# An attention and expert kernel whose recorded order of operations is replaced by one meant to keep VectorE's shared-port steps clear of GpSimd's steps

## Chip, cores, metric

One core of one Trainium2 chip. The metric is device time of one execution in microseconds (us); lower is better. Kernel before: 264.78 us, median of 3 runs (264.57 to 265.2).

## The reference, cut to what matters

```python
mod = (silu(c) @ w_mod).reshape(1, 6, 1, 576)            # sa, ca, ga, sb, cb, gb
h = layernorm(x) * (1 + ca) + sa                          # x: 1 x 2048 x 576
# 32 heads of width 18, 4 segments of 512 tokens:
for s in range(4):
    p = softmax(qs @ ks.T * scale + causal_mask)          # exponentials on ACT
    a_mem = (phi(qs) @ M) / (phi(qs) @ z + 1e-6)          # phi(t) = t + 1 if t > 0 else exp(t)
    o = g * a_mem + (1 - g) * (p @ vs)
    M, z = M + phi(ks).T @ vs, z + phi(ks).sum()
x = x + ga * (o @ wo)
h = layernorm(x) * (1 + cb) + sb
r = h @ w_r;  best = argmax(r)                            # one token of 2048 goes to the expert
y = (silu(h[best] @ w_gate) * (h[best] @ w_up)) @ w_down * sigmoid(r[best])
out = x + gb * (h + scatter(best, y))
```

Attention fills most of the time; the expert on one token (weights of 576 x 4608) is the tail, because the token is known only when all 2048 have been scored.

## The kernel before: the parts that matter

The kernel first writes down some 1650 operations with what they read and write, then emits them in a recorded order. A number in that order says which operation comes next and which of its alternatives (engines) is taken. Semaphores follow from what is read and written; nothing but its place in its own engine's queue keeps an operation back when its data is there.

```python
    def recorded(self):
        raw = base64.b85decode(BANKS)
        for g, b in zip(self.groups(), raw):              # PSUM banks of each group
            g.banks = [b] if g.n == 1 else [b // 8, b % 8]
        raw = base64.b85decode(ORDER)
        seq = []
        for x in struct.unpack("<%dH" % (len(raw) // 2), raw):
            o = self.ops[x // 4]
            o.eng, _, o.emit = o.alts[x % 4]              # x % 4: the engine chosen
            seq.append(o)
        return seq
```

The steps in dispute, all between operands in SBUF:

```python
    def tt(out_, a_, b_, o_, R, W, pool=False):           # residual and modulation steps
        if pool:
            return op(one("POOL", 1.3, lambda: nc.gpsimd.tensor_tensor(...)), ...)           # L912
        op(alts(("DVE", ..., lambda: nc.vector.tensor_tensor(out=out_, in0=a_, in1=b_, op=o_)),    # L913
                ("POOL", 1.3, lambda: nc.gpsimd.tensor_tensor(out=out_, in0=a_, in1=b_, op=o_))))  # L914
    ...
    ts_ = ...tensor_scalar(PH, QT, 1.0, 1.0, op0=ALU.add, op1=ALU.max)   # L698, VectorE, one SBUF input
    mn_ = ...tensor_tensor(out=PH, in0=PH, in1=EQK, op=ALU.min)          # L700, VectorE, two SBUF inputs
    # L559: normalisation on VectorE (L558 on GpSimd); L931: sum of the two attention parts
    # L787: affine_select, GpSimd, causal mask on the exponentials (L776, ACT)
```

In the tail, `xcols` (L1240 to L1242, three VectorE steps of up to 6 columns) makes the input of the expert's matmuls (L1259) from what the selecting matmuls left in PSUM.

## Time and profile before

| before | value | where it is read |
|---|---|---|
| time | 264.78 us (264.57 to 265.2) | the runs |
| span of the profiled run, mean granted clock of PE | 264.4 us, 0.928 | the list of cores |
| first exponential starts, last ends | 32.6, 234.8 us | L776 in ACT's timeline |
| ACT idle between them | 20.9 us of 202.3 | the same |
| VectorE port steps held by over 0.1 us | 31 of 87, 20.0 us in sum | each step's time less the fastest of its shape |
| of that on the chain that ended last | 9.6 us (from 144.7 us on) | chain of waits |
| PE at half clock | 38.3 us in 7 stretches | granted clock, within the span |

"Port steps" are VectorE's steps between operands in SBUF. A step's held time is its time less the fastest of its line and shape; "on the chain" is what of that lies on the chain of work that ended last. "Half clock" is time with a granted TensorE clock of 0.50. "Held" and "on the chain" are worked out by one rule for all kernels here, the fastest being taken over both kernels; by the prediction's rule, which took the kernel before alone, the first is 19.5 us.

For the comparison I cut the span in four at the work, not at the clock: up to the first exponential, to the 113th of 160, to the end of the last, and the rest. These are the busy times of the kernel before by those stretches (start and end of the stretch, its length, then busy us and instructions of PE, PE loads, VectorE, ACT, GpSimd; granted clock; DMA share; GB/s):

```profile
0.00:32.60 32.60, 27.78 (x225) 14.28 (x228) 22.91 (x87) 12.37 (x24) 13.17 (x38) 0.84 0.77 217
32.60:169.70 137.10, 130.19 (x1836) 76.90 (x1852) 119.80 (x268) 130.19 (x158) 87.34 (x109) 1.00 0.58 183
169.70:234.80 65.10, 54.88 (x1098) 34.33 (x1098) 57.18 (x144) 51.10 (x62) 45.73 (x72) 0.84 0.62 185
234.80:264.40 29.60, 19.46 (x386) 12.10 (x385) 17.37 (x68) 6.65 (x19) 14.21 (x23) 0.87 0.59 209
```

The profiled run took 266.25 us, 1.5 over the median. The second stretch is ACT's: 130.2 of 137.1 us. In the third no engine is full; VectorE comes nearest, with 57.2 of 65.1 us, 9.1 of them held.

### The profile page before, as it was taken

What the parts mean: (1) busy time and instruction counts of PE and PEld (TensorE: products, weight loads), DVE (VectorE), ACT (ScalarE), POOL (GpSimd) and SP (SyncE); (2) the same over time, 40 slices, a digit from 0 to 9 for tenths busy, and PEclk for the clock granted to TensorE, in tenths of its full rate; (3) what the DMA queues carried; (4) which work ended last, traced back from release to release, by engine and by line L of the source; (5) the groups of instructions that cost most, each with busy time, mean ns of one, the idle gap of its engine ahead of it and who ended that gap; (6) DMA issues with size and microseconds to landing.
All of it is one profiled execution on the core that took longest, in us unless ns stands there. A gap on an engine that the chain in (4) does not pass through costs nothing. (4 is left out here: it accounts for less than half of the span.)

```text
span 264.4 us, 8893 instructions
## 1 busy us (share of the span) xinstructions
PE 232.3 (88%) x3543; PEld 137.6 (52%) x3562; DVE 217.3 (82%) x564; ACT 200.3 (76%) x257; POOL 160.5 (61%) x240
## 2 busy tenths in 40 slices
...
ACT  2232999999997988999999999968757995774020
...
PEclk9858999999999999999999999997777995899689
...
GB/s 172 321 186 273 142 222 124 149 233 259 139 183 150 146 100 247 110 145 141 139 152 327 252 132 260 249 135 137 210 219 49 271 260 191 135 297 298 140 326 3
DMA packets 35263, 50.38 MB, mean 191 GB/s; under 512 B 4043, under 2 KB 29266, under 8 KB 35222
## 3 DMA queue, kind: packets, MB, share of 16 engines
...
q10 hardware_dynamic: 544, 0.59, 0.7%
...
HBM read 37.93 MB, written 11.87 MB: 188 GB/s over the span
## 5 line engine op out<-in xcount | busy, mean ns | idle before, releaser
L776 ACT ACTIVATE arena<-PS 128x1024 bf16<-128x1024 f32 x160 | 152.3, 1037 | 11.5 <-PE PS L758 6.6
L787 POOL TENSOR_SCALAR_AFFINE_SELECT arena<-arena 128x1024 bf16<-128x1024 bf16 (+1 forms) x59 | 57.6, 987 | 47.5 <-ACT arena L776 45.5
L645 PE MATMUL PS<-arena 128*128 128x512 bf16 (+1 forms) x176 | 50.9, 391 | 1.5 <-issue 0.9
L758 PE MATMUL PS<-arena 18*128 18x128 bf16 (+2 forms) x736 | 37.7, 266 | 3.2 <-DVE arena L810 0.9
L950 PE MATMUL PS<-arena 128*128 128x288 bf16 x160 | 30.3, 313 | 2.0 <-DVE arena L943 1.0
L758 PEld LDWEIGHTS <-arena 18*128 18x128 bf16 x736 | 16.1, 94 | 26.6 <-issue 23.7
L802 PE MATMUL PS<-arena 128*32 128x128 bf16 (+2 forms) x736 | 25.5, 269 | 4.3 <-issue 2.5
L712 PE MATMUL PS<-arena 128*128 128x288 bf16 x160 | 28.1, 292 | 0.3 <-issue 0.2
L914 POOL TENSOR_TENSOR arena<-arena 128x576 bf16<-128x576 bf16 x20 | 26.5, 1329 | 2.4 <-DVE arena L913 1.9
L645 PEld LDWEIGHTS <-arena 128*128 128x128 bf16 (+1 forms) x195 | 17.8, 103 | 16.8 <-issue 6.0
L802 PEld LDWEIGHTS <-arena 128*32 128x32 bf16 x736 | 14.3, 98 | 14.9 <-issue 8.5
L551 POOL TENSOR_TENSOR mv<-mv,epsF 128x1 f32<-128x1 f32 (+2 forms) x21 | 4.1, 194 | 26.9 <-DVE mv L544 25.9
L558 POOL TENSOR_SCALAR arena<-arena,rstd,nmr 128x576 bf16<-128x576 bf16 x19 | 17.0, 897 | 5.4 <-DMA arena<-in_A_x_dram 4.5
L649 DVE CAST arena<-PS 128x512 bf16<-128x512 f32 (+1 forms) x26 | 17.5, 681 | 3.1 <-DMA arena<-in_A_x_dram 1.1
L950 PEld LDWEIGHTS <-arena 128*128 128x128 bf16 x160 | 14.9, 105 | 9.3 <-issue 1.9
L810 DVE CAST arena<-PS 128x512 bf16<-128x512 f32 (+1 forms) x26 | 17.2, 663 | 1.9 <-PE PS L802 1.6
L913 DVE TENSOR_TENSOR arena<-arena 128x576 bf16<-128x576 bf16 x25 | 18.0, 736 | 0.1
L712 PEld LDWEIGHTS <-arena 128*128 128x128 bf16 x160 | 13.8, 98 | 7.6 <-issue 2.2
L542 DVE BATCH_NORM_STATS2 st<-arena 128x6 f32<-128x288 bf16 x30 | 13.6, 452 | 4.6 <-DMA arena<-in_A_x_dram 4.5
L964 DVE SCALAR_TENSOR_TENSOR arena<-PS,arena 128x288 bf16<-128x288 f32 x32 | 14.2, 447 | 3.3 <-PE PS L953 3.1
L695 ACT ACTIVATE arena<-arena 128x1024 bf16<-128x1024 bf16 (+1 forms) x18 | 16.6, 924 | 0.0
L552 POOL TENSOR_TENSOR rstd<-mv,mhalf 128x1 f32<-128x1 f32 (+2 forms) x21 | 13.5, 644 | 4.2 <-DVE mhalf L407 2.7
...
## 6 DMA issues: line engine op xcount, KB each, us to landing
...
```

Of the source, the lines that this page charges most:

```text
L558: a = {"POOL": ("POOL", 0.83, lambda: nc.gpsimd.tensor_scalar(dst, src, sc_, bi_, op0=ALU.mult, op1=ALU.add)), "DVE": ("DVE", 0.43, lambda ...
L645: nc.tensor.matmul(bank(g, 0)[0:r], lhsT=lhs(k), rhs=h1T[hb][:, k, :], start=(k == 0), stop=(k == KC - 1))
L649: op(alts(("DVE", dv(512, "P"), lambda g=g, dst=dst, r=r: nc.vector.tensor_copy(dst, bank(g, 0)[0:r])), ("ACT", ac(512), lambda g=g, dst=d ...
L712: nc.tensor.matmul(bank(g, 0)[:, 0:288], lhsT=h1T[hb][:, k, 128 * b:128 * b + 128], rhs=WP["v"][:, k, 288 * hf:288 * hf + 288], start=(k = ...
L758: nc.tensor.matmul(bank(gs_[x // 2], x % 2)[:, off:off + b - a], lhsT=KS[32 * x:32 * x + DH, c, 128 * j:128 * j + 128], rhs=QS[32 * x:32 * ...
L776: op(one("ACT", 1.035, lambda g=gs_[x], pt=pt: nc.scalar.activation(pt, pair(g), ACT.Exp, scale=SCALE)), R=[("lt", n)], W=[("PT", pp, x)], ...
L787: om = op(alts(("POOL", 0.68 if pat[0][1] == 4 else 1.12, lambda v4=v4, pat=pat: nc.gpsimd.affine_select(out=v4, in_=v4, pattern=pat, comp ...
L802: nc.tensor.matmul(bank(gp, 0)[32 * x:32 * x + 32, o0 + a - qa:o0 + b - qa], lhsT=va[:, j, 4 * c + x, :], rhs=PT[:, pp, x, off:off + b - a ...
L810: ("DVE", dv(w, "P"), lambda gp=gp, ai=ai, gi=gi: nc.vector.tensor_copy(ASB[ai][:, gi, 0:w], bank(gp, 0)[:, 0:w]))),
L913: op(alts(("DVE", dv(576, acc=2), lambda: nc.vector.tensor_tensor(out=out_, in0=a_, in1=b_, op=o_)), ("POOL", 1.3, lambda: nc.gpsimd.tenso ...
L914: ("POOL", 1.3, lambda: nc.gpsimd.tensor_tensor(out=out_, in0=a_, in1=b_, op=o_))), R=R, W=W, lock=True)
L950: nc.tensor.matmul(bank(g2[hf], 0)[:, 0:288], lhsT=ot[:, k, :], rhs=wop[:, k, 288 * hf:288 * hf + 288], start=(k == 0), stop=False)
```

## The change

Its intent: order all operations so that no VectorE step that uses the port shared with GpSimd is due while a GpSimd step runs. Only the two tables change; of the operations common to both, 151 also change engine (117 of them are five masks, five steps on GpSimd that become 112 small matmuls on PE; 34 are others), the PSUM banks change, and 55 filling matmuls become 44. The tables cannot be read by eye:

```diff
 ORDER = (
-    "001-qOaKS~cmO;A&;Wn{lmM6j<p2Z#gaLp7Pyh@7d;rw|Z~$BY*#I~IKmnWpi~$e;XaH0Iv;n*UxB=||%mJVPqyVS@hyjcMumF$&lmVClzyZVo$N|s+gaAbV"
     ... (34 more lines out)
+    "00A@rOaM>-cmP}g=m2m4d;kalgaPCL3;>J)Kmd>dJOESxfC01txB<KY%mI`E1OPYzH~`Q9U;vl_005i-hykDgqyP{A%mAnWAOOGt$N{hb#Q`t?)Bw-{6aZuZ"
     ... (all lines of the table new)
 BANKS = (
     ... (9 lines changed)
```

More of the change, by code (lines that the diff above doesn't have):

```diff
@@ L35 @@
 ORDER = (
-    "001-qOaKS~cmO;A&;Wn{lmM6j<p2Z#gaLp7Pyh@7d;rw|Z~$BY*#I~IKmnWpi~$e;XaH0Iv;n*UxB=||%mJVPqyVS@hyjcMumF$&lmVClzyZVo$N|s+gaAbV"
-    "K>!p0xB$EWtN@$=+ySHkpaH-D=>YHm^Z<weU;yv|SODw+v;g%1I02{uAOK_lpaawaumRWs7zf}1paM7o=>cd0%m91=+yIaO<pBf(+yZO@AP2+%JObbXPy(a_"
-    "xC00StOGCrqykg|r~;@1umeB>90#oe$N*RZMFOk=a0284bpl-iBnMyu3<HD$7y|eK90CyoxB_?r=>qHm2m&Aiv;zzR_yQCIB?9~ayaU7oC<4F(5CTX7C<puj"
-    "ECK)m6#_5<1p?3m$ODK1OaqJpYydR^_ybS_WCP#;8~~95AOlnbFb8M@00d+LBm+zW*aQ3nZ38?3EC)0P+yf{Bhyy?almkQq-~&kmm;;>yj05NcI0r-r>;v!v"
@@ L40 @@
-    "!~$>w$O0?_kpp}K%mVZS1Oz<?fCC5wlmbBqTn9-9umXhx3<P`v&;now5Cmig<O56xPzP8CbOU$;SOe4oNB~s_Tm$$3oB~J$C;(ss00C?Vv<z?uzzk>ybO%rb"
-    "m;xvSfC5Ye90^neybLV_SOg#mTm-xVxC~$fBni+5zyf#(83Z5%6a@SNd<duq)Ca^2fCwA}I0J+T*axf!XaukaFaz8NB?Qn6Gy{+av<Ex`Fa&S}Yy^k|ln2QS"
-    "*aDCQ^b8mSH3Vb?_y?E=j08LcI0VfMbOiVeoCp03v;sf`{0Ddh;0Htm1Oe~@fCS6~m;{{!cn5q0@CTp>bN~Pd1PG)E*aY+f)C|}R;0zQ9d<X0Ypa-Z37zp$S"
-    "+zi|VhzNuPfCq#J-~^Netq8aTyad1qpaj4K!~_5XEC3_`=nVJ><P01L<OEa*r34`eL=wmZJQ7$4tOV=~KoY0~%miEr7y$eT&;+;#)C8~u2m$d7BnSZs)B|7$"
@@ L44 @@
-    "v;+(R7y;-6@C57x;0Txn<Omc2oCSyn2nFZ}C<QPD4FwznFbJRps09!KECr+mGzhE(_yqg}I0#V^JP5D_v;_bK7!7O)a0na$BmwLQ1PSy6O%fapKnNfKR1!D^"
-    "JOv;P1O-e15D6p=C;=!9@CXzM2nqBEbO<mFKn27H3<(egNCh|&Gz~Nb6$MNMSPf7G$OnuE7zxY=NC7wvxDB`kNC><Q#0AI&JPlX{m<UV=zy)OiECEOoPzYQN"
-    "U<JSp&;`5&%mrW#)CDjBWDTSTj0ju>01ccCya+S_Xa#TuWC%nB1PyEjbOpo>01hk&)Cf=kKn(~8#0X#kpbfkS*a(ye=n8xi2n|>P-3Z7C><VlFY!b`}coNYF"
-    "bPdQ2R0XgIqz!NZkO-*_1P<^D^a^MVfDLH@3=L=!_zGMSoCsJFff6VNbO9g>2oC%TVG<|~<Og^GbrOUP3=4=2ObuiO3=Sv@WD>LzB@5^Wzz1*=Eej9}6bp?F"
@@ L48 @@
-    "EDit*1Pd?@H4YdHkPR>k2n!txcm*g4cnviR+zr$XxDrqeeFfkRFbNP2d=0!3I0-BX5D4TAfCa!3oD!@J=nXsxg$4KxKnYY0^bH^m><x$oNE3_&NC`{{kOh<l"
-    "pb|s~OcOK-q!OqSqz)Vf7zI!XAO%DTs1DE#XbCVA5DichG!twIC<r743<wAqa0#pqR0(tmv<OracnMeuTnRW6NDJ5vU<o`6*adwFI13CIKnp|*JQFMpObZ+i"
-    "Y!g%q+y&qTtP*4is0pwMEC#p;Fb1p%a1;CufC<P6g$Z;MTn>y0&<S7;coWzO%n4);hzTSP>;>cn+zIdn;0cfklnGD^=mh`<nF%xoXb3z8^aY>^{RKD%_yxHM"
-    "2nL)9I1WVyzzMVolnqD*)Cs%^#R)(LPzK})r3pw53<iu26b(cUh!c<wj1$NPO$Jy7C<>Jh=m~rVkP~<Y?FoPe6caECFdPU9Q~@js3<@*~7!wc*5e66rs1TGB"
@@ L52 @@
-    "tPmU%@CmRD#1i!hTm~ElArr6=j0QjxND5F2ObYlCkOo)_U<R}hd=sDs{1R9bR0f>}7zzLrgc8gK1QQ$zR0@a^I0_&N&<0Qrj1pW6NDW*8kP?^^m<@ymBnngx"
-    "JPKG2Kne&G%ngVJcnTB>m<Id__z8Rp019XhxDad(bPfaxl?Fr#SPFm&ybxdtaSo^oTnexX)CPDCs0L*UtP0o$m=1gnxC$T!L=Bt{a19g&@C{53X$HUwZ3YAe"
-    "pbpRy)DpA`m<reuyb9<BoC<^rtOlS8<p$ga;0B2bkP5^Kj0$WG+!CM=?FRS;U<;%Ql?v<<XbON1Yznjugbwfqhz`&Su@1NnloI>~^ai95)e6W8v<@^JI2=42"
-    "zz)a`%?jKK*a~n8bP7NmL>x#QOdL=g&<?N$;0ojl#17C9WD95uYzrg?%n&>d3=H%a+z`kR#1PaD_!j^N@D4x@*bcxDWCr*S<QHHJ2?x{=%no=9;1X~Py$-kr"
@@ L56 @@
-    ";SPKYBolB3^bUy&bPEj!=nmWt<PPl)j0?;cfeQc+Ko3X{{0@W*L=U6}xeI&{fDnWbyasdz6b`ftR2;kua1eA5$Pxq(Fb{YT2oE?9zzYozU=R2c{1X5a)Dx5o"
-    "02mk!G!JACArIISXb;^JBoCMph!Bhr%nK+FEe|{okPy%d;0xUgzy??xTpUmj5Dyd&7!Sk?R1e4tkPi?C=n@<c*bvwY2n<94)eD#loeNA4uo7?&SPz&FY!3_*"
-    "U>vXybr0+lln>+*Tn_{o#0KaK><hFH@DuzO%o2DH@C)<{!4DJ%xDWIb5Da|}fDaT5#1F_1gb%zEoDZZ6h!5lopbx+kqz{Y_#1mW$WDFn-WE=nxXbdC_Gz`2C"
-    "F$}2-s1Fzn1P~ky(GRo+tPkK1`3nRG2oTs0DGaa^EDSsh<qx0>)DIvKv=g`!-48$v%?~6HtqTkgln^Kom=Nd>oDg&jXdDp`U=#fd0Sp)r?GNx0MGVjvYz!<A"
@@ L60 @@
-    "6cBg}WD|u9a11dJL=!X+I1q>o@DGp+^bc$ta2#|TK@da`ToX(T$P<7J9S}$m_zzJG{0~qN1Ppx)kPPS$RS+-~I24QwG!)De&=ar=C=>J&O%Od0SP)$h1QZ|?"
-    "Bot^9lngu(2o!`9WDpP&U=R!xcpQ8j5fnHKXb@}=><}mv6cpeSoD8HB<P+!<NDP1+fE1_`@DQLA7!(~8h!o%u<Pf9`^bn{FgdB(*j2r+F1QApWU=%DApbUf*"
-    "lo9w4XcVjyOcp#85fKy-K@m_EWEA`mR2D!ML>534oD(b)j1)u^a1;p<*cV6^m=Qz~coeM+=@D!cWEMyioDmEWbQF9PND*ijY!*xu5E#G|#1u>s$P`o&P!Zr4"
-    "kP#daSP^Iu7!h0%AQ9vdWf8CxxD>P$%oJ1<U=dIhkQ7)HToh~(>=9TDm=q)tfD@DyoD}g9C=pl|kQ~tza1qoLTozy!+!v%2ED@*?pcJSS*c7Z0)E6NYC>5*}"
@@ L64 @@
-    "m<*s1q!GLnxe)*ryb&Z7>=!K+@D~Ub-4t{Yc@gvxv=Olp1QqBMF%hr~_z@8mG!cLi?G)e?Ko}Gi^b`mZ3>Ewl1rit)9Tnvi@DyPc#1Z%u{1h-1=ofquWEE%?"
-    "H5C975E2a%Z52@!6c{)a#1=gjSQS7OR23K!lpL5GL=~JBpcP0JOch-fg%NZW$PsWAcom!+pd6$ej1_Peq!oY_bQX9P$QH~N%n{HLd=)qm)e(Fah!zwQ*b&?j"
-    "fEI)m&=!;xkQE>oh!u<$7#P42m==i<j1im`gcjftkQUe#91<WB;1wJfBp2Kj)E3+p*cOx);1=u_Bod$&s1<k@C>O~U%oU^-<rXOtm=*9A=oa`E<Q1?LtQDvn"
-    "tQ@c$1s2d12o~%W3>Nejs20@~=oPgU@f9o=5f&sExD~t=6&4s4z!e-8#1$|XAr|x%{1yNg_!TG^ED{742p9Yn02VYCNEl2QKo?LLd>1SjI2S}0Bo-(ZR2Z}z"
@@ L68 @@
-    "fEP#?EEY5tFcvr#JQq9`g%_+ASQs%9h!>F;loy#7To|wxj2BQBR2K~wU>KYiq!+jss289YtQS}pTo=3-uot)-yd1zB#2m;R%p7bOz!!uV#23gH&>Ykp*c{v("
-    ";2h)}=p1kubQob5>>ThM^c?sc{2Txs1RZ=BfEW-LI2h;{G#E4zco;+&WEf}|q!_doxE4$o6c@Y}JQ!pbv=;~+oEV50z!oqVpct$es2Cg=AQ)*E>=^VIZ5Qwu"
-    "j2IXfkQkI0a2IqJ_!#^cuo$!$xEQ<`z!=0B%oxxZ$Qaxh*cj9p;27i>02u@s2pO0d3>g")
-BANKS = (
-    "2LK8N2L%8J1O^2H00RaG0S5yI0S5p80R{jHB?=`sB@-naE(Zq(6D1`994;;a0WJap1OYAzE&(njHxnfR2LLw{0VO2?0WKT?0S5vD1OWjY1_c5H009F71p);H"
-    "0R{jE0s#jE1ONa60|W;E2Ll2F1~(iW0Rbfe6AC2<1_L)769E$?B>^`90ssOf6E_?IB{u;I90dXaB{v*5Hwpna95(<40099v0RjdB03`+m1O*2N2Lb~E0|EjE"
-    "0|f>K0t5yJ0s;d90ssU81_B2YB{wA#B>^`RHv$3z0UQB0Hyi;j95(_40UQA(H!cA#6E`IT0|F%h0XGUIB{u;j2Lu2d0WLQH0S5sA0tW&D0s{mB0|NsG1qTBK"
-    "1_b~B1_lEM2LJ#D0tW{L2MQb$E&&q+0|o&cE&(n92Lb{m0VOvjHvj+zHzf)s0VM<k0xkgo69)$_0RbEU023|&E(Ze&911rB023|&0RjR90|x{H1q25I00#g8"
-    "0RaF32R8sE0RR91000000000000000000000000000000000000000000000000000000000000000000000000000000000000000000000000000000000"
+    "00A@rOaM>-cmP}g=m2m4d;kalgaPCL3;>J)Kmd>dJOESxfC01txB<KY%mI`E1OPYzH~`Q9U;vl_005i-hykDgqyP{A%mAnWAOOGt$N{hb#Q`t?)Bw-{6aZuZ"
@@ new lines @@
+    "fB>ujgaGgWqyg{&>;aqsL;&mnJONk$v;f!vpaHl5)B*JY+yUSLPy+k_hybVo<N??KgaT*+paa|h+yaaMI0C!?zyQPm$N=B~d;w?xBnRmM-~ylmKmoV|1OXri"
+    "umP+AkN{Ky90!O3qyjtw<N~MyYyzzUKmu?Abpludi~{rk!~z%xqyt?72m+A;7y_sRMFO}2_yMc~cmfOpumijU`~mm?5CXshlmh7j$O8ZZ1p;6K90C;rNCGGV"
+    "AOb7`=mRAJFao>+$N~fd!~-Y?%mOR`fC2~uAOl1J_yW)ZoB}lhOad$ilmqMo@B<73m;?9&v;#l`L<1xPWC9Tbd;-)0oC7om`~#Q*83aiKhy#oR8~`u}^aIQT"
+    "C<E*Q00bNaAOw&DECV<Pd;{16fCGdBWCPp-XanE_Yy$`cKnF|%5Cm8QJO^+CumVK~3<OXEzye7JbOT%iU<Y^uB?Mdt1Ozk#<O37~NCa#LR0CiGXa`UPa0g@u"
@@ new lines @@
+    "Oax2^xC}4@PzMwQC<HJBR0k{s5E-}xzyw$a&;zIkI0UQ*bO$vAzzjG8JOr=@Km@!5L<D#Q*aEZ%fCLBud<3)t3;}2aYy?>Za0I*z6aoAKkO!0i_y}ACU<8-|"
+    "ln0mxi3E%UJOgC}kOY+k00R&KYyflw{0OuRoCg32R0Nm=)C1rMBml?+$qdW{pa+Bm#01a;<OrPv&<yAZcnF{b)C3p-=mhKpr3CN<d<ex1907O-&<A`6^a6kg"
+    "fCq&L*aRp5-~`+R5DC-=ga^$G*bLYQ+y~SQ6bRi6;0$yC_yimStOWD~7y~E)s08o=umrROxCa;r<OKW#00oE#ECD0|6bTp!90(x@BnaRKya)IUj0Xq>NCor^"
+    "1O*KR<P01M_y<r0Oa+(){0!&}@CTd)5Cv!jGy(hv><1tT@C<AP><kqJBnbcra0LVi^alh97!4QzL=rFvI0Y~PumuPSC<w#{Gzhc>JOw}n91RQ!I0#q;JP05S"
@@ new lines @@
+    "NB|@apaozBqy<z6s0APatOaxhSO{DNR0ZS*C<QD9$Ol{qFa=-;YzSomqz9k~7zJbnqzF|K90ec+KoWojXbD6GBn2=Hg#|PPs0cI-ObDz9KnQFJDG59ha0ze-"
+    "I1M}vcm+@r2nZ|*m<ZerI0@hlFbTK~%m?HRH3`TF=m&iThy`>AbP0?FWC%P7=nZrMhzLLlun3R^%m~m3NC`v;><GLKzz38Cj0h+V3<yXFbPm`B@CZx^zzw(s"
+    "zy-twPzX>7^aw-=lnBHPOcGcL$OT*poCwGb&;?WpU<teh)ChPE%mvs8C=O5o01cQ4ya)shOaZ_MSOH)G><ugq2n`Gkd=A|R3>ee}fDN1p5D2&kcnN3-pb2CN"
+    "eF>-u#0YQ!Obs{^unB|>APXc5Fb;?fEC`GZfC)7YYypJ{tO?i&;0fFXXaQIa^a?-?+zDI_-~|{9U=8>RxCsyq9Si&l=nA|EzzJjxoDGNxpbd}>j0vO-sSWH3"
@@ new lines @@
+    "@CwKY&<T(Ucmb3NECxstFa}r>ToQN^#0h*7ff8s9I1Y>s%n4u;3=5D5v<YMqEDaC~Fbm`fGz*Xpm<|*RC=09&l@6Q^p$?=8EDKN#2nrAi3<>}X1PeF|L<@Kg"
+    "NDJ%*2n*;5R1I_u7z#WK?FnoR@CAGg912tmKnv6f@Cg(OObZ|i)D6%LP!4DklnwO>R1P=_KniRUSPlRNL=EHx&=Rx==mjJSGzNSIJPLFYC<ZtN{RMaiNCEf-"
+    "aT4_fMFu<uNCqehfd)VZ)DkQTgc48-2nJ0CSO(Y<L<(37Tnh{aTn3yHFbYrxh!Qjkv<-L)pc35@5e5ht{0XEIs1o=IfC`KfY!i?Y01f~Od<p~#ND9~ufDQx>"
+    "^bN=c_zg@7gbsuXPzq=c2oA6fa1Cq@NE56Qi4O1$6b%dxSPEPLaSj{~83r5%Tnb?ZXa@WZm<lixOcNjupb9h-oC<IgI1_{hR0cc~NDdGVhzd{>;1X05R0@a&"
@@ new lines @@
+    "j0OY-m<?DHqzXh1bQ6pUm<CJ^kOrLwQ~{6*U<x4ylm?&%lnP`9xC#^#c@xYAWeOM*Yzoi@6b`@&+y<xyyb3%H#0p3aXbNx&sS2<PbPB8n_!8g-loBKk922Yx"
+    "wF*EJAQSu&U=!^I@CM8c$O_B~&<Z3Ium%(cU<=R=pb*sxxdy!k029;>q!8E+*b3YV;0ojl;1kpa<P+%=*aid>zz)O?Weep7=mszxa1f*pZ3c7@$PTa&v<9dS"
+    "co4M^7!Irs2os19unr^!3=E7AkPxU4%nsZRTn@MnKn}DHU=FMhVGLvr@DB72^ai*Pybx#$m=gF7uoAQqybkyVAP*=HBoDX}Yzw>+{04Cb00+Pla0}oL=neo6"
+    "1rOv7cnfq3Ko6t_<QIGkEDwPT$Pk1Jd=tPBL=Q+0#1POB%n-N>ybFj6{0<Nd)DXlH<PzKvFb}X31P8zd><$zR2n;k2zzYZubOzuMI1h{q2nUo4U=Oqth!czx"
@@ new lines @@
+    "WDo2UkQ2BQv<qkt>=H~54G)wP@DubCd=SVIJP%M0R1XaY%nN`J=n`-b&<lhR{1<f(m=mB65C>Qf;0ve^-3!DEqz}Xf$P>s5kq^uhY!A>Em=D+sTnyC<APkfb"
+    "To0HF&=YtMoeR(p*bfv3Bn;>aGz>5dWDN8d7z}6(tPj)=91MI9u@96Gr3>r}_!A5hv=68Y%o6+)oewMwDGU$~m=N#_+z%`hI1HQ+xDON$7!QyO0Tg5t!4Gr{"
+    "cnri3$PdjAy$=Bp2oTH{1P~k#`3tQJ{R@Q*5EF<DC==ih=npXvG!Q%tI1ud*)DzefL=*55Ko9^7*bwv!<qtp%+!OQ?JrHOUfDc3vYz&|as1rmCunU9_ND$}{"
+    "h!2bpa18ht5D*v;ToZi^6c8a04G^3Y1Pmw;JP{-iEf7r%91u(pfD8l_@DGp-2o$^%^bf!j<PZ!L1Q-w$7!;%vP!RYJ#1s4vSP&ExaTHY$T@ZK_pcAYUbQE9^"
```

18 lines of the change are left out of this document (17 added, 1 removed).

## The prediction

> **What bounds the kernel now.** I read the page first (engine shares, slices), then the groups by shape, then the chain that ended last, then the timelines of VectorE and GpSimd where that chain runs through them.
>
> ```profile
> PE 232.3 (88%) x3543; PEld 137.6 (52%) x3562; DVE 217.3 (82%) x564; ACT 200.3 (76%) x257; POOL 160.5 (61%) x240
> ACT  2232999999997988999999999968757995774020
> PEclk9858999999999999999999999997777995899689
> ```
>
> No engine is full over the whole span, but ACT is full from slice 5 to slice 27 (6.6 us each: 33 to 178 us), where it works through 160 exponentials of the attention. In that part a faster VectorE is worth little. From slice 27 on ACT falls to 5 to 7 tenths and the granted clock to 0.7: something else paces the work. The first exponential starts at 32.6 us and the last ends at 234.8 us; ACT is busy 181.4 of these 202.3 us, so at most 20.9 us could come out of this part. The tail after it is 29.6 us.
>
> Groups by shape, where a mean far over the fastest one of the same shape gives away waiting inside the instruction:
>
> ```profile
> L913 DVE TENSOR_TENSOR arena<-arena 128x576 bf16<-128x576 bf16 x25 | 18.0, 736 | 0.1
> L698 DVE TENSOR_SCALAR arena<-arena 126x1024 bf16<-126x1024 bf16 x12 | 8.3, 703 | 0.0
> L914 POOL TENSOR_TENSOR arena<-arena 128x576 bf16<-128x576 bf16 x20 | 26.5, 1329 | 2.4 <-DVE arena L913 1.9
> ```
>
> The same L913 add or multiply takes 440 ns at its fastest, 459 at the median and 1519 at its slowest; L698 takes 409 to 1410. These are the SBUF-to-SBUF steps of VectorE (L913, L931, L698, L700, L559 and four single ones: 87 in all). Against the fastest of the same shape, 31 of the 87 are held by over 0.1 us, 19.5 us together. VectorE evictions from PSUM (L810, L649) keep within 10% of their fastest. The chain and the timelines show what holds them:
>
> ```profile
> 172.15 1.06 DVE arena L698
> 173.39 1.38 DVE arena L559
> 174.77 1.23 DVE arena L698
> ...
> 187.62 0.44 DVE arena L913
> ...
> 188.39 2.38 DVE arena L913 x2
> 190.77 1.45 DVE arena L931
> 192.22 1.42 DVE arena L700
> ```
>
> ```profile
> 189.35 1.11 POOL L787 TENSOR_SCALAR_AFFINE_SELECT arena<-arena 128x1024 bf16<-128x1024 bf16 x1 [0.16 <-ACT arena L776]
> 190.44 1.47 POOL L914 TENSOR_TENSOR arena<-arena 128x576 bf16<-128x576 bf16 x1
> 191.87 1.48 POOL L931 TENSOR_TENSOR arena<-arena 128x576 bf16<-128x576 bf16 x1
> ```
>
> Between 188 and 194 us VectorE and GpSimd alternate: each VectorE step ends about 0.2 us after the start of the next GpSimd step, so a 0.44 us step lasts as long as the GpSimd step it waited for. PE starves meanwhile (it waits 2.7 us for VectorE before 176.8 us) and its clock is halved at once:
>
> ```profile
> 178.40:181.80 3.40, 3.40 (x45) 1.30 (x46) 2.66 (x8) 2.71 (x3) 1.48 (x5) 0.51 0.36 101
> ...
> 195.40:202.20 6.80, 6.64 (x60) 3.84 (x59) 4.71 (x14) 5.20 (x7) 2.76 (x5) 0.50 0.34 131
> ```
>
> (Columns: stretch and its length, busy of PE, PE loads, VectorE, ACT, GpSimd, granted clock, DMA share, GB/s.) The same happens in the tail, where VectorE's queue delays the input of the expert's matmuls:
>
> ```profile
> 245.54 0.38 DVE arena L913
> ...
> 245.94 3.23 DVE arena L913 x3
> 249.17 0.07 DVE arena L1240
> ...
> 249.58 5.94 PE PS L1259 x96
> ```
>
> What L1240 needs was done when PE ended L1235, at 246.2 us; it started at 249.1 us because three L913 stand before it in VectorE's queue.
>
> **What the Trainium skill says.** "SBUF — State Buffer", section "Who interferes with whom": a VectorE instruction in a 2-port mode contends with GpSimd, one with two SBUF inputs contends with a GpSimd instruction that reads SBUF, whoever issues first has the shared pair for the whole instruction and the other fully blocks; PSUM-source steps in single-port modes do not. The trace agrees: 440 against up to 1519 ns for the SBUF steps, and nothing alike for the evictions. A GpSimd memset beside L559 at 242.1 us costs it under 0.04 us. "TensorE: Matmul & The Clock Gate", Part 1: an idle window of about 3.4 us halves the clock. The trace has stretches at 0.50 after the VectorE pile-ups, as shown.
>
> **The change part by part.** The program of operations is the same; only the recorded order, the choice of engine where there are two, and the PSUM banks differ. From the built orders, with the durations of the trace before:
> - VectorE loses 7 memsets to GpSimd (5 x 0.485 + 0.9 + 0.3 = 3.6 us) and three elementwise steps (3 x 0.44 = 1.3), three x1 copies of L962 (3 x 0.45 = 1.3) and a 0.4 us copy to ACT; it gains four L636 (4 x 0.54 = 2.1), three L718 (1.4) and two L878 (0.9) from ACT. Sum: about -2.2 us.
> - ACT: -4 x 0.77 - 3 x 0.42 - 2 x 0.65 + 3 x 0.41 + 0.4 = -4.0 us of 200.
> - GpSimd: +7.7 us (5 x 0.61 and about 1.2 of memsets, one norm 0.8, two tensor steps 2.6) and five masks fewer (2 x 1.16 + 3 x 0.68 = -4.4): +3.3 us.
> - PE: those five masks as 112 small matmuls (7 blocks of 16, about 0.16 us a block as 16 of L767 show on the chain: +1.1), 11 fill matmuls fewer. No sum here exceeds 2% of the span: if the change gains, it is by order.
> - Order: VectorE's 87 port steps become 84. 50 of them stand in runs of two and more before, 39 after; 23 have no other VectorE step between them and the GpSimd step before them in the recorded order, after it 17. So the crowding falls, by a quarter or so, but does not vanish on paper.
>
> What is it worth? Going through the held steps that lie on the chain, and counting only the time over the fastest of their shape: 9.3 us on VectorE (172 to 175 us: 2.4; 188 to 194: 3.6; 144 to 147: 1.2; tail: 2.1) and 1.1 us on GpSimd, 10.4 us. The chain reaches back to 144.7 us only; the 6 us held before that lie beside a full ACT and I count none of it. I take 60% of the 10.4 as saved, 6.2 us: the order is only a plan, as no semaphore keeps a GpSimd step back until VectorE is done, and a GpSimd step whose data is ready starts when its queue reaches it. In the tail one can see this: the four L913 still stand before L1240, and the first of them releases an L914 on GpSimd, which can again fall between the others. The planned removal is worth 2.4 us there (L1240 at about 246.8); I expect half. To this I add 1.3 us for PE: five half-speed stretches after 178 us make 27.3 us; if one of 3.4 us goes where PE was the pace, that gives back 1.7 us, and I discount it. Sum: 264.8 - 6.2 - 1.3 = 257.3 us.
>
> The start should stay: 27 against 21 GpSimd operations and 44 against 48 of VectorE come before the first exponential, and the DMA-fed projections set it.
>
> **The rivals.**
> 1. The wait moves rather than goes. GpSimd, or PE with its 88%, fills the gap, or steps that were spaced out to avoid the port now come late for their readers. For it: PE is at 9 tenths nearly throughout; GpSimd's own work grows. Against: PE's tenths include matmuls that only wait, and between 171 and 178.4 us it is busy 4.7 of 7.4 us. That would leave 261 to 265 us.
> 2. The plan does not survive on the chip: collisions stay at about 25 of 84, since start times are not enforced. For it: the modest fall in crowding counted above. Then about 262 us.
> 3. The order as a whole is better. ACT's side work is spread: before, 17 other ACT operations stand between exponentials 40 and 50, after the change at most 8 in any such ten; 33 fill matmuls stand between first and last exponential before, 13 after, so the plan has fewer PE holes. If ACT's idle of 20.9 us fell to 8 and the tail gained 2.4: about 249 us.
> 4. New order, bad luck: a load or a PSUM bank comes late in a place that no count shows. 265 to 268 us.
>
> **Range and chances.** Rivals 2 and 1 bound the range above, 3 below: 257.3 us, with 250 to 264 holding it 8 times in 10. Faster by 2% means under 259.5 us, which needs half of the 10.4 us: 0.62. Within 2%: 0.33. Slower: 0.05, as the known waits only shrink.
>
> **What would show it.** Right: L913's mean down from 736 to 500 to 600 ns, held steps from 31 to 12 to 18, their sum from 19.5 to 7 to 10 us; ACT at 8 to 9 tenths between 178 and 230 us; fewer half-clock stretches; L1240 within 1.5 us of the end of L1235. Wrong: the held sum falls below 8 us but the span stays over 262 us (rival 1), or the sum stays over 15 us (rival 2), or the span drops below 250 us with the held sum unchanged (rival 3).

## The result and the profile after

| | before | changed, first profile | changed, second profile |
|---|---|---|---|
| median of the runs, us | 264.68 | 251.97 (249.12 to 252.43) | 252.04 (251.49 to 253.7) |
| span, us; mean clock | 264.4; 0.928 | 247.0; 0.971 | 250.1; 0.957 |
| first exponential | 32.6 | 29.3 | 31.3 |
| last exponential ends | 234.8 | 219.3 | 222.4 |
| ACT idle between | 20.9 | 10.4 | 11.3 |
| port steps held, sum | 31 of 87, 20.0 | 22 of 84, 11.0 | 22 of 84, 10.5 |
| of it on the chain | 9.6 | 2.9 | 4.1 |
| half clock, us | 38.3 | 14.4 | 21.4 |

Ratio of the fast runs, changed over before: 0.9493, 95% interval 0.9433 to 0.9554. Two more runs of the changed kernel took 251.37 us and 254.33. A run is slow when it is over 1.5% above the fastest of its kernel. Ratios in this document are the mean time of one kernel's fast runs over that of the other's fast runs in the same rounds, in the experiments without the profiled run, so they are not quite the ratio of the medians quoted, which take in slow runs. Half clock varies without the change: b_tail below, whose order is the old one up to the tail, had 28.5 us of it. The first profile of the changed kernel caught its fastest run, so I rest on the second, a median run taken with the experiments.

The page of the changed kernel (first profile), ACT and clock in 40 slices, here of 6.2 us:

```profile
ACT  3123999999799999999989899999888999964030
PEclk9979999999999999999999999999979999999589
```

ACT now stays at 8 to 9 tenths until slice 34, near the end of its exponentials; the hole in slices 27 to 33 has closed. Groups by shape of the same kernel:

```profile
L913 DVE TENSOR_TENSOR arena<-arena 128x576 bf16<-128x576 bf16 x24 | 12.6, 535 | 0.2
L698 DVE TENSOR_SCALAR arena<-arena 126x1024 bf16<-126x1024 bf16 x12 | 5.9, 490 | 0.0
L914 POOL TENSOR_TENSOR arena<-arena 128x576 bf16<-128x576 bf16 x21 | 27.5, 1315 | 2.8 <-DVE arena L913 2.1 <-DVE arena L559 0.2
```

L913 fell from 736 to 535 ns a step (fastest 440 before, 395 after), L698 from 703 to 490; GpSimd's own L914 stayed at 1.3 us. By stretches of the same work as above (second profile):

```profile
0.00:31.30 31.30, 28.03 (x225) 13.89 (x226) 21.30 (x80) 11.50 (x21) 15.91 (x42) 0.89 0.82 235
31.30:167.80 136.50, 132.42 (x1879) 78.77 (x1877) 119.00 (x275) 130.45 (x156) 95.08 (x118) 0.99 0.57 173
167.80:222.40 54.60, 48.06 (x1167) 33.24 (x1166) 49.91 (x142) 49.30 (x61) 40.90 (x67) 0.94 0.81 249
222.40:250.10 27.70, 19.88 (x394) 12.84 (x394) 17.20 (x66) 6.08 (x18) 10.02 (x20) 0.92 0.62 210
```

Of the 14.3 us between the two spans, 1.3 lie in the start, 0.6 in the stretch that ACT fills, 10.5 in the third (65.1 to 54.6) and 1.9 in the tail. In the third, VectorE's time divides like this: held 9.1 to 2.6 us (-6.5), idle 65.1 - 57.2 = 7.9 to 54.6 - 49.9 = 4.7 us (-3.2), and work 48.1 to 47.3 us (-0.8). So by this account a good half of the gain there is the port, but not all: VectorE also waits less for others. (The kernel before is not an odd profile here: b_tail, unaltered in this stretch, has 65.2 us.)

The start. The first normalisation needs `rstd` (L552), and L552 a constant, `mhalf`. Timeline of the kernel before, then of the changed one (first profile; start, duration, what, and the wait before it):

```profile
8.94 0.06 DVE L407 MEMSET mhalf<- 128x4 f32 x1
9.15 0.72 POOL L552 TENSOR_TENSOR rstd<-mv,mhalf 128x2 f32<-128x2 f32 x1 [2.65 <-DVE mhalf L407]
...
11.93 0.29 PE L628 MATMUL PS<-arena 128*128 128x128 bf16 x1 [3.00 <-POOL arena L558]
```

```profile
5.76 0.06 DVE L407 MEMSET mhalf<- 128x4 f32 x1
...
7.22 0.72 POOL L552 TENSOR_TENSOR rstd<-mv,mhalf 128x2 f32<-128x2 f32 x1
```

Before, the 60 ns memset stood behind some twenty others in VectorE's queue; GpSimd waited 2.65 us for it and PE 3.00 us, and PE's clock then stayed halved from 11.1 to 21.3 us. After, it is set 3.2 us earlier and the transposes start at 9.2 us. In the two profiles of the changed kernel half speed at the start lasts 3.4 and 6.8 us, and the first exponential comes at 29.3 and 31.3: the start differs by 2 us from run to run. Twelve kept profiles have one start or the other. In them the first exponential goes with the half-speed time at the start: 28.6 to 29.7 us where that is 3.4 us (five, all with the new start), 31.1 to 31.9 where it is 6.8 (four with the old start, two with the new), 32.6 where it is 10.2 (the kernel before, this profile alone). So the new start seems to help mainly by more often keeping PE's clock up; no run changed the clock there by itself. The Trainium skill says so of the clock ("TensorE: Matmul & The Clock Gate", Part 1: its activity window is free-running, so a kernel's slow stretch varies from run to run), and the two profiles agree.

The tail, on the chain of the changed kernel (first profile; start, duration, what):

```profile
230.03 1.43 DVE arena L913
...
231.48 0.46 DVE arena L913
231.94 0.07 DVE arena L1240
...
232.35 5.89 PE PS L1259 x90
```

L1235 ended at 230.8 us (L1223, which L1240 waits for, 0.4 us earlier). L1240 comes 1.1 us later (2.9 before), behind two L913, one of which is held 1.0 us. The expert's first matmuls take 5.9 us as before, still at half clock.

### The profile page after: what moved, and what is told of

Its sections match the earlier page's. It is cut to its first block, busy times and chain, and to the rows that moved or that the text cites. A ratio compares the mean times of both kernels' runs of the same rounds, so it can differ in the third digit from the quotient of the medians.

```text
span 247.0 us, 9116 instructions
## 1 busy us (share of the span) xinstructions
PE 224.8 (91%) x3663; PEld 137.4 (56%) x3663; DVE 206.8 (84%) x559; ACT 197.1 (80%) x252; POOL 162.3 (66%) x245
## 4 chain that ended last, share of the span: by engine, by line
PE 35%; DVE 13%; DMA 9%; ACT 9%; issue 2%; SPq 0%; DVEq 0%; ACTq 0%
ACT arena L776 7%; PE PS L645 6%; PE PS L758 5%; DMA arena<-k_d 4%; PE PS L950 4%; DMA arena<-q_d 3%; PE PS L802 3%; PE PS L712 3%; PE PS L1259 3%; PE PS L888 2%; DMA arena<-in_B_w_gate_dram 2%; DVE arena L913 2%; PE PS L821 1%; PE PS L939 1%; DVE arena L964 1%
## 5 line engine op out<-in xcount | busy, mean ns | idle before, releaser
L776 ACT ACTIVATE arena<-PS 128x1024 bf16<-128x1024 f32 x160 | 153.0, 1038 | 8.9 <-PE PS L758 5.0
L787 POOL TENSOR_SCALAR_AFFINE_SELECT arena<-arena 128x1024 bf16<-128x1024 bf16 (+1 forms) x54 | 52.8, 990 | 39.5 <-ACT arena L776 39.4
L645 PE MATMUL PS<-arena 128*128 128x512 bf16 (+1 forms) x195 | 53.4, 384 | 0.1
L758 PE MATMUL PS<-arena 18*128 18x128 bf16 (+2 forms) x736 | 37.4, 259 | 7.5 <-ACT arena L776 1.8
L758 PEld LDWEIGHTS <-arena 18*128 18x128 bf16 x736 | 17.1, 92 | 28.2 <-issue 22.5
L950 PE MATMUL PS<-arena 128*128 128x288 bf16 x160 | 29.4, 296 | 0.6 <-DVE arena L943 0.2
L914 POOL TENSOR_TENSOR arena<-arena 128x576 bf16<-128x576 bf16 x21 | 27.5, 1315 | 2.8 <-DVE arena L913 2.1
L712 PE MATMUL PS<-arena 128*128 128x288 bf16 x160 | 27.3, 287 | 0.7 <-DVE arena L832 0.4
L802 PE MATMUL PS<-arena 128*32 128x128 bf16 (+2 forms) x736 | 23.4, 260 | 0.3 <-DVE arena L832 0.3
L558 POOL TENSOR_SCALAR arena<-arena,rstd,nmr 128x576 bf16<-128x576 bf16 x20 | 17.9, 898 | 4.7 <-DMA arena<-in_A_x_dram 3.6
L950 PEld LDWEIGHTS <-arena 128*128 128x128 bf16 x160 | 14.0, 100 | 7.7 <-issue 1.5
L712 PEld LDWEIGHTS <-arena 128*128 128x128 bf16 x160 | 13.7, 97 | 7.9 <-issue 2.6
L542 DVE BATCH_NORM_STATS2 st<-arena 128x6 f32<-128x288 bf16 x30 | 14.1, 470 | 1.9 <-DMA arena<-in_A_x_dram 1.9
L552 POOL TENSOR_TENSOR rstd<-mv,mhalf 128x1 f32<-128x1 f32 (+2 forms) x21 | 13.7, 652 | 1.6
L964 DVE SCALAR_TENSOR_TENSOR arena<-PS,arena 128x288 bf16<-128x288 f32 x32 | 14.2, 444 | 0.4 <-PE PS L953 0.2
L650 ACT CAST arena<-PS 128x512 bf16<-128x512 f32 (+1 forms) x17 | 9.6, 589 | 5.2 <-PE PS L645 5.0
```

The source lines that it names most:

```text
L558: a = {"POOL": ("POOL", 0.83, lambda: nc.gpsimd.tensor_scalar(dst, src, sc_, bi_, op0=ALU.mult, op1=ALU.add)), "DVE": ("DVE", 0.43, lambda ...
L645: nc.tensor.matmul(bank(g, 0)[0:r], lhsT=lhs(k), rhs=h1T[hb][:, k, :], start=(k == 0), stop=(k == KC - 1))
L712: nc.tensor.matmul(bank(g, 0)[:, 0:288], lhsT=h1T[hb][:, k, 128 * b:128 * b + 128], rhs=WP["v"][:, k, 288 * hf:288 * hf + 288], start=(k = ...
L758: nc.tensor.matmul(bank(gs_[x // 2], x % 2)[:, off:off + b - a], lhsT=KS[32 * x:32 * x + DH, c, 128 * j:128 * j + 128], rhs=QS[32 * x:32 * ...
L776: op(one("ACT", 1.035, lambda g=gs_[x], pt=pt: nc.scalar.activation(pt, pair(g), ACT.Exp, scale=SCALE)), R=[("lt", n)], W=[("PT", pp, x)], ...
L787: om = op(alts(("POOL", 0.68 if pat[0][1] == 4 else 1.12, lambda v4=v4, pat=pat: nc.gpsimd.affine_select(out=v4, in_=v4, pattern=pat, comp ...
```

## Experiments

The theory before them: the time came from the port (theory A), plus the earlier start; rivals: PE's half-speed stretches, the place of L1240, the choice of engines, and an order better in itself. The first four were run together on one chip (before: 264.94 us, median of 7 runs), the next four on another (before: 265.06, 9 runs from 261.0 to 268.19), the last four on a third (before: 265.81, 11 runs). Where a set's own fastest run of the kernel before lies far out, some others count as slow and the verdict reads unclear; I therefore give medians of all runs beside ratios; where the two differ, the ratio of fast runs is the fairer one. Each kernel but the write-only ones gave the right result.

### b_start: the kernel before with the changed start

```diff
  # kernel before; in the recorded order
- 166 operations ahead of the first exponential, in the old order
+ the same operations in the changed kernel's order and on its engines (9 change engine)
```

> Before, with the operations ahead of the first exponential in the order (and on the engines) of the changed kernel; all later ones as before. Theory A (a good part of the gain is not the port at all but the start: in the kernel before, the GpSimd chain of the first layer norm waits 2.65 us for a memset of mhalf far back in VectorE's queue, PE idles 3.0 us and is then held at half clock from 11.1 to 21.3 us): first exponential near 29.5 us instead of 32.6, half-clock time at the start 3.4 us instead of 10.2, and 3 us or so off the time: 261 to 262.5. Theory B (the gain is the port, later on): the start is absorbed later, 264 to 265.

Measured: 262.77 us (261.16 to 265.63), ratio 0.9968 (0.9874 to 1.0063). The profile has the first exponential at 28.8 us, half speed at the start only 3.4 us, and all else as before: 32 steps held, 20.4 us, third stretch 63.4 us, tail 30.0. The start is worth about 2 us by the medians, 0.8 by the ratio, and the interval holds zero.

### b_tail: L1240 to L1242 moved up in the kernel before

```diff
  # VectorE and PE queues, kernel before
- ... L1305/1306, L1212, L913 x4, [PE L1223, L1235], L1240-1242
+ ... L1305/1306, L1212, [PE L1223, L1235], L1240-1242, L913 x4
```

> Before, with L1240 to L1242 (the expert's input) put ahead of the last four L913 in VectorE's queue; nothing else. If the two L913 held there by GpSimd are on the path as I read them: L1240 starts within 0.3 us of the end of PE L1235 instead of 3 us after it, and 2 to 3 us come off: 262 to 263. Rival (the expert's weights or another load pace the tail): no change, 264.5.

Measured: 264.66 us (263.19 to 266.21), ratio 0.9994 (0.9903 to 1.0085). L1240 did come at 247.2 us, as soon as L1223 had ended and before the end of L1235, but L1235 itself ended 1.4 us later (247.6 against 246.2). The timeline shows why:

```profile
245.27 1.32 DVE L1306 SCALAR_TENSOR_TENSOR arena<-arena 1x1 uint32<-1x1 f32 x1
245.32 1.27 POOL L914 TENSOR_TENSOR arena<-arena 128x576 bf16<-128x576 bf16 x1
...
246.53 0.14 DVE L1212 TENSOR_TENSOR arena<-arena 1x1 bf16<-1x1 f32 x1
```

A step on one element, 0.21 us in the kernel before, lasts as long as the GpSimd step beside it, and L1212, which the last selecting matmuls need, stands behind it. The wait moved from a large step to a tiny one.

### b_fill: filling matmuls in PE's longest waits of the kernel before

```diff
  # PE queue, kernel before
+ 52 more filling matmuls (L1351) in the four longest waits after 170 us (19 + 7 + 8 + 18)
```

> Before, with 52 more fill matmuls (19, 7, 8, 18) placed in PE's four longest waits after 170 us, which keep the array active and compute nothing. All port collisions stay. If half-speed stretches after the pile-ups are a large term by themselves (before has 20.4 us of them between 178 and 226 us, after 3.4): they vanish and 3 to 6 us come off, 259 to 262, with the held sum still near 19 us. Rival (PE's clock does not matter there because VectorE paces): under 1.5 us, 263.5 to 265.

Measured: 267.4 us (264.41 to 272.39), ratio 1.0107 (1.0 to 1.0215). The same window of the kernel before and of this one (columns as above):

```profile
178.00:226.00 48.00, 41.06 (x762) 24.70 (x751) 40.94 (x99) 35.98 (x43) 34.62 (x55) 0.79 0.63 184
```

```profile
178.00:226.00 48.00, 40.79 (x801) 26.80 (x786) 41.32 (x103) 37.78 (x46) 34.29 (x55) 0.93 0.64 188
```

The mean clock rose from 0.79 to 0.93 (half-speed stretches there 20.4 to 6.8 us), while VectorE did as much as before and no time was gained (two of the four runs were slow, at 268.57 and 272.39). Part of that rise may be chance. The same window of b_tail, in which nothing was altered:

```profile
178.00:226.00 48.00, 38.40 (x784) 24.09 (x787) 41.79 (x98) 36.18 (x44) 34.74 (x55) 0.87 0.64 184
```

That is 12.6 us of half speed against 20.4 in the kernel before, and the last exponential ended at 234.8 us in both kernels. Filled or by chance, less half speed did not bring the end forward: the slow clock between 178 and 226 us is a sign that PE is kept waiting, not what costs the time.

### b_write: GpSimd's large steps made write-only in the kernel before (result wrong)

```diff
+    def w2(o, a, b, f):
+        nc.gpsimd.tensor_tensor(out=o[:, 0:2], in0=a[:, 0:2], in1=b[:, 0:2], op=f)
+        nc.gpsimd.memset(o[:, 2:], 0.0)
+        nc.gpsimd.memset(o[:, 2:], 0.0)
...
-                ("POOL", 1.3, lambda: nc.gpsimd.tensor_tensor(out=out_, in0=a_, in1=b_, op=o_))), R=R, W=W, lock=True)
+                ("POOL", 1.3, lambda: w2(out_, a_, b_, o_))), R=R, W=W, lock=True)
# the same for L912, L931, L558 and L787: two columns read, the rest written by memset
```

> Before, same order, with GpSimd's large steps (masks, norms, products and sums) replaced by a 2-column step of the same kind plus memsets that fill the rest of the same destination: same waits, nearly the same length, but almost no SBUF reads. The result is wrong on purpose. Theory port: two-input VectorE steps (L913, L931, L700) are no longer held, the held sum falls from 19.5 to under 8 us (L698 and L559, in a 2-port mode, may still be held), and 7 to 11 us come off: 254 to 258. Rival (GpSimd's length and PE pace, not the port): over 261 us.

Measured: 255.23 us (253.36 to 255.85), ratio 0.9633 (0.955 to 0.9715); relative error 0.61. GpSimd's busy time is as before (160.7 against 160.5 us), so only what it reads has changed. Groups of this kernel by shape (its L918 is L913, its L703 is L698):

```profile
L918 DVE TENSOR_TENSOR arena<-arena 128x576 bf16<-128x576 bf16 x25 | 10.8, 448 | 1.1 <-POOL arena L328 1.0
L703 DVE TENSOR_SCALAR arena<-arena 126x1024 bf16<-126x1024 bf16 x12 | 6.8, 578 | 0.0
```

L913 is at 448 ns and held 0 times in 25 (11 before), L931 once in 9 by 0.1 us, L700 twice in 18 (5 before); L698 is still held 6 times in 18 (7 before) and L559 3 in 13, as before. In sum 14 steps and 5.8 us are held, 0.7 on the chain. So 9.7 us (264.94 - 255.23) come from the port in the old order, without moving anything. In the third stretch held time fell from 9.1 to 1.9 us but the stretch only from 65.1 to 60.0: VectorE was then idle for 10.1 us of it instead of 7.9. An order made for other times does not fill the time that it is given.

The Trainium skill ("SBUF — State Buffer", section "Who interferes with whom") says that a VectorE step with two SBUF inputs contends with a GpSimd step that reads SBUF and not with one that only writes, while a 2-port step (a `tensor_scalar` can be one) contends either way. This run agrees: the steps with two inputs (L913, L931, L700) came free, the `tensor_scalar` steps (L698, L559) hardly did. An L698 (L703 here) at 96.3 us is held by 0.33 us with nothing but a memset beside it, so the prediction's one memset that cost L559 under 0.04 us was no rule.

### after2: the changed kernel again

Unaltered, so there is no edit.

> The changed kernel again, unaltered, on the same chip as the three that follow. Both theories: 252 us, within 1.5 us, ratio to the kernel before about 0.95. It is the yardstick of this set.

Measured: 252.04 us (251.49 to 253.7), ratio 0.958 (0.9493 to 0.9666). It repeats.

### a_write: the changed kernel with write-only GpSimd steps (result wrong)

```diff
  # changed kernel
- GpSimd's large steps
+ the same write-only steps as in b_write
```

> The changed order with GpSimd's large steps turned into write-only ones (result wrong on purpose). In its profile the changed kernel still has 22 VectorE port steps held, 11.0 us, but only 2.9 us of that on the chain. Theory A (the order took out nearly all of the collisions that matter): 249 to 251 us, a gain of 1 to 3 us on the changed kernel run beside it, held time under 5 us. Theory B (what is left of the collisions still sets the time): 4 us or more are gained, below 248 us.

Measured: 248.47 us (245.61 to 252.0), ratio 0.9369 (0.9268 to 0.947). By medians that is 3.6 us less than the changed kernel beside it, between the two theories. But three of the six runs are slow; the three fast ones have a mean of 246.7 us, and by the ratios (0.958 - 0.9369, times 265 us) the gain is 5.6 us: theory B, what is left of the collisions still costs. The profiled run (252.0 us, slow) has 9 steps held, 4.1 us, 0.8 on the chain. What paces the fast runs was not profiled.

### b_startwrite: changed start and write-only steps in the kernel before (result wrong)

```diff
  # kernel before
+ the edit of b_start
+ the edit of b_write
```

> The kernel before with the changed kernel's start and with write-only GpSimd steps (result wrong on purpose): neither the new order of the middle nor of the tail. Theory A (the change's 12.7 us are the port plus the earlier start): the two gains measured alone, 9.7 and about 2, add up, to 252 to 254 us, the changed kernel's time within 2 us. Theory B (the new order is worth something in itself, apart from the port): it stays above 255 us. Theory C (the start's gain is lost again in the middle, as it was when tried alone): 255 us, the same as with the write-only steps alone.

Measured: 253.25 us (252.23 to 255.01), ratio 0.9607 (0.9529 to 0.9686). The gains add up (265.06 - 253.25 = 11.8, against 9.7 and 2.2 alone), 1.2 us short of the changed kernel. Theory A by its number. But the four kernels together say more. Medians in us:

| | port in play | GpSimd write-only | what the port costs |
|---|---|---|---|
| old order, changed start | 262.8 (b_start) | 253.25 (b_startwrite) | 9.5 |
| changed order | 252.0 (after2) | 248.5 (a_write) | 3.6 |
| what the order gives | 10.7 | 4.8 | |

By these medians the new order removes 9.5 - 3.6 = 5.9 us of the port's cost, still pays 3.6 of it, and gives 4.8 us that are there even with GpSimd's reads out of the way. By the ratios of fast runs, each to the kernel before of its own set and times 265 us, the port costs 9.6 us in the old order (0.9968 - 0.9607) and 5.6 in the new (0.958 - 0.9369), so 4.0 are removed, and 6.3 us (0.9607 - 0.9369) are the order's without the reads. Each ratio is known to about 0.01, or 2.6 us: the 6.3 are clear of zero, the 4.0 by themselves are not. That the port's cost did fall rests also on the held time on the chain (9.6 to 2.9 and 4.1 us). (b_start is of the first set, the other three of the second; the kernel before was 264.94 and 265.06 in them. The write-only kernels keep some held steps, so both costs of the port are a little low.)

### a_tail: L1240 to L1242 moved up in the changed kernel

```diff
  # VectorE and PE queues, changed kernel
- ... L1215, L913 x4 (with L1234, L1212 and [PE L1223, L1235] among and after them), L1240-1242
+ ... L1215, L1234, L1212, [PE L1223, L1235], L1240-1242, L913 x4
```

> The changed kernel with VectorE's three small L1240 to L1242 steps put ahead of the last four L913 tiles of its queue; result must be right. In the changed kernel they come 1.1 us after the last L1235 step has ended, behind an L913 held 1.4 us. Theory A (the tail's chain runs through L1235 and L1240): L1240 starts within 0.3 us of L1235's end, and 1.0 to 1.5 us are gained on the changed kernel beside it, about 250.7 us. Theory B (as in the same move on the kernel before: another small VectorE step of the chain is held instead, or the PE runs at half clock just the same): within 0.5 us of the changed kernel.

Measured: 251.0 us (247.74 to 252.03), ratio 0.9485 (0.9362 to 0.9609). Four of its five runs lie below the lowest of the changed kernel beside it (251.49), the medians 1.0 us apart; the intervals of the two ratios overlap. L1240 starts when L1223 ends, 0.2 us before the end of L1235 (theory A), and from the last exponential's end to the expert's first matmul it takes 11.9 us instead of 13.1. Part of that was given back further on:

```profile
237.43 3.99 POOL L912 TENSOR_TENSOR arena<-arena 128x576 bf16<-128x576 bf16 x3 [3.21 <-DVE arena L1277]
...
239.16 0.94 DVE L1293 TENSOR_SCALAR arena<-arena 128x36 f32<-128x36 f32 x1 [1.76 <-ACT arena L1290]
...
243.92 0.31 DVE L1326 TENSOR_TENSOR arena<-arena,ug 128x144 f32<-128x144 bf16 x1 [1.90 <-DMA ug<-u_d]
```

L1293, 0.18 us in the changed kernel, is held until the second of three L912 ends; in this run the chain goes on from it to the gather whose row L1326 waits for. Again a small step took over the wait.

### a_start: the changed kernel with the old start

```diff
  # changed kernel; in the recorded order
- 167 operations ahead of the first exponential, in the changed order
+ the same in the order and on the engines of the kernel before
```

> The changed kernel with everything ahead of the first exponential in the order and on the engines of the kernel before; result must be right. Undoes the part that was tried alone on the kernel before (there it gave 2.2 us, with an interval that holds zero). Theory A (the start is worth its 2 to 3 us whatever follows): first exponential 2 to 4 us later, at 32 to 33 us, half-speed clock of 7 us or more at the start, and 254 to 255 us. Theory B (a later start is taken up by slack in the middle, since ACT has 10 us of idle time there): within 0.7 us of the changed kernel, 252 us.

Measured: 258.79 us (256.55 to 261.87), ratio 0.9752 (0.9705 to 0.9799): 6.8 us over the changed kernel's 252.0 of the other set, neither theory's number. First exponential at 31.1 us, no later than in after2. The loss lies at the seam:

```profile
45.76 0.54 PE L758 MATMUL PS<-arena 18*128 18x512 bf16 x4 [3.91 <-DMA arena<-q_d]
```

PE waits 3.9 us and ACT, for PE, 4.0 us for a queue round trip; in that window a 1152 KB load of `w_mod` was issued on the same queue, which stood elsewhere in both parents. My splice made a new order of transfers; that the load caused the wait was not tested. So this run says nothing clean about the start. It does show that even the start's order is bound up with what follows.

### b_alts: the old order with the changed engines

```diff
  # kernel before
- 151 operations on the old engine (or mask)
+ the same 151 at their old places on the engine of the changed kernel
```

> The order of the kernel before with the engine that the changed kernel gives each operation (151 change engine, none moves); result must be right. With the port out of play on both sides the new order was still 4.8 us faster than the old (248.5 against 253.25, write-only GpSimd steps), so something besides the port was gained. Theory A (it is the engine choices: less on ACT and VectorE, masks moved off PE): 258 to 261 us. Theory B (it is the order itself): the engine choices alone, set for another order, give nothing or cost something: 263 us or more, and 25 or more port steps held.

Measured: 313.5 us (311.13 to 316.92), ratio 1.1765 (1.1707 to 1.1822). Theory A is out: the engine choices give nothing by themselves. Yet not for the reason that B gave: only 22 steps are held, 14.1 us, fewer than before. What grew are plain waits of engines for one another (all waits of this kernel: who, for whom, us in total, times, longest):

```profile
ACT arena L776 <- PE PS L758: 21.7, 17, 5.3
ACT arena L776 <- PE PS L767: 17.0, 15, 3.9
```

In the kernel before, L776 waits 6.6 us for L758 in all. ACT is idle for 68.5 us between first and last exponential.

### a_alts: the changed order with the old engines

```diff
  # changed kernel
- 151 operations on the changed engine (or mask)
+ the same 151 at their changed places on the engine of the kernel before
```

> The converse: the changed kernel's order with each operation on the engine of the kernel before; result must be right. If the avoidance lies in order and engines together, as the intent says, old engines at the new places bring collisions back. Theory A (order alone carries the gain): 253 to 256 us, at most 24 port steps held. Theory B (order and engines only work as a pair): 259 us or more, 27 or more held.

Measured: 286.3 us (285.47 to 286.95), ratio 1.0764 (1.0727 to 1.0801). Theory B by its time (259 or more); its count (27) was just missed with 26 steps and 17.5 us held, 4.4 on the chain, and ACT idle for 40.5 us. Order and engines hold only as a pair (the PSUM banks, the third part of the change, stayed those of the order in both runs and were never tried alone), and the number of collisions does not rank these kernels: 286 and 313 us have less held time than 265.

### a_tailfill: the tail move with filling matmuls

```diff
  # a_tail
+ 7 filling matmuls ahead of the last search (L1208), 5 ahead of L1214
```

> The changed kernel with L1240 to L1242 moved up (as in the run before, which gave 251.0 against 252.0) and 12 fill matmuls on PE in the tail, so that its clock is full when the expert's 96 matmuls run; result must be right. In that run the matmuls still took a stretch of 3.4 us at half speed. Theory A (the stretch is set by PE's idle time before it, and the tail waits on PE): no half-speed stretch between 225 and 240 us, the 96 matmuls in under 4.8 us (5.9 in the changed kernel), 249 to 250 us. Theory B (the fills themselves sit in the chain, or the clock stays half all the same, as with the fills in the kernel before): 251 us or more.

Measured: 252.18 us (250.78 to 255.69), ratio 0.9455 (0.9412 to 0.9498). The expert's 96 matmuls do run at full clock:

```profile
236.68 4.08 PE L1259 MATMUL PS<-arena 128*32 128x512 bf16 x96
```

4.08 us instead of 5.7 to 5.9. A half-speed stretch remained before them, from 226.2 to 229.6 us, so theory A's sign came half true. And the first half of theory A does not carry the second: no gain on a_tail is shown. In the profiled run (slow) PE then waits 1.31 us for the first `w_down` piece before L1337, and VectorE 3.21 us for the gather. Against the kernel before of its own set it is 13.6 us faster by medians, a_tail 14.1 and the changed kernel 13.0 (by ratios, times 265 us, 14.4, 13.6 and 11.1), within what the sets scatter.

The best correct versions here are a_tail and a_tailfill, which these runs do not tell apart. a_tail is 1.0 us under the changed kernel beside it by medians and 2.5 by ratios, which is not clear of the noise.

## Why the prediction was right or wrong, by its steps

The side (faster by over 2%) and the range were right; the value, 257.3, was 5.3 us too high.

- **VectorE paces after 178 us, ACT before: right.** (It puts all 160 exponentials before 178 us; it is 118.) Of 14.3 us, 10.5 came after the 113th exponential and 0.6 in the stretch that ACT fills. Counting the early holds as worth nothing was right for the new order (8.7 to 6.8 us held there); b_write shows that they are not quite free (8.7 to 3.9 us held, 137.1 to 134.7 us long).
- **6.2 us from the chain's holds: right, as far as the runs can tell.** On the chain 9.6 us fell to 2.9 and 4.1 in two profiles, so 5.5 to 6.7 went; the four kernels with and without GpSimd's reads say 5.9 by medians and 4.0 by fast runs.
- **60%, since nothing enforces the plan: about right.** 22 steps are still held, and a_write takes 3.6 us more off (5.6 by fast runs). Of the port's cost 5.9 of 9.5 us went by medians, 4.0 of 9.6 by fast runs. The counts given, 12 to 18 held and 7 to 10 us, were somewhat too hopeful (22; 10.5 to 11.0); L913's mean (500 to 600) was 535.
- **1.3 us for PE's clock: not borne out as a gain of its own.** b_fill took 13.6 us of half speed out of 178 to 226 us and gained nothing, and b_tail had 7.8 us less of it than the kernel before with the same end. That the stretches fell because PE waited less was not tested alone. The prediction quotes from the Trainium skill that an idle window of about 3.4 us halves the clock. Less was enough here. In the 3.4 us before the half-speed stretch at 178.3 us PE was busy for 1.5, and before one of the changed kernel's (second profile, 139.9 us) for 2.4, with no wait over 0.73 us.
- **"The start should stay": wrong.** I counted operations and did not look at what the first of them waited for: a 60 ns constant, and PE idle for 3.00 us. First exponential 1.3 to 3.2 us earlier; 2.2 us by medians when tried alone (0.8 by the ratio), with an interval that holds zero.
- **Tail, half of 2.4 us: right in size.** (The prediction names L1235 as what L1240 needs; it is L1223, which ended 0.2 us earlier in the kernel before.) L1240 came 1.1 and 1.3 us after L1235 instead of 2.9; the tail is 1.8 and 1.9 us shorter.
- **"If the change gains, it is by order": half of it.** No sum of engine choices exceeded 2%, true; but the order without its engines is 286 us. They cannot be told apart.
- **The missing term** is what rival 3 named: the order better as a whole. ACT's idle fell from 20.9 to 10.4 and 11.3 us (rival 3: 8), and 4.8 us (6.3 by fast runs) remain with GpSimd's reads out of play. I gave that rival as the low end of the range instead of adding part of it to the sum.

By the medians the gain of 12.9 us (264.94 to 252.04) then reads: start 2.2, port 5.9, order and engines (with the banks) apart from the port 4.8. By the ratios of fast runs it is 11.1 us: 0.8, 4.0 and 6.3. Either way the three add up because of how they are formed, and the first is weak. Which of the last two is larger is not shown. What the last is made of stays open: part is VectorE's idle time in the third stretch (7.9 to 4.7 us), but no run undid one such wait alone.

## What to carry to other kernels

Take from held steps only what lies on the chain, but when an order is made anew as a whole, also ask what the engines' plain waits would gain: here that was about as much as the collisions. Clearing a large step from in front of a critical one helps only until the next tiny step of the chain meets a GpSimd step, so check every VectorE step of the chain for SBUF operands, down to one element. An order and the engine of each operation are one thing: to test a part, remove what makes it wait (here GpSimd's reads), since splicing two orders brings waits of its own.

## What the Trainium skill lacked or had wrong

- "SBUF — State Buffer", "Who interferes with whom", gives no size under which contention can be ignored. Tiny steps were held here too: a two-input step on one element took 1.32 instead of 0.21 us beside L914, and a `tensor_scalar` on 36 float32 columns 0.94 instead of 0.18 us beside L912.
- The same section advises on contention, but no page says what it is worth. Here 20.0 us of held time had 9.6 us on the chain, and taking 14.2 us of it away gained 9.7 us; two kernels with less held time (17.5 and 14.1 us) were slower by 21 and 48 us.
- "TensorE: Matmul & The Clock Gate", Part 1, does not tell when keeping PE warm pays. Half speed between 178 and 226 us cut from 20.4 to 6.8 us gained nothing, and an expert stage brought from about 5.8 to 4.08 us gained nothing measurable either. Nor does it tell how much idle time slows the clock: before two half-speed stretches PE was busy 1.5 and 2.4 of the last 3.4 us.
